# The rows of v go out behind the decay rows and the raw rows, in every item's step

## The chip, the cores and the metric

One core of a Trainium2 chip runs the whole program in one launch. The figure of merit is the device time of one execution in microseconds. The kernel before took 563.85 us (median of three runs, 561.96 to 565.06). TensorE (PE) multiplies, VectorE (DVE), ScalarE (ACT) and GpSimd (POOL) work elementwise, and SyncE (SP) does nothing here but issue transfers (DMAs).

## The reference

Causal attention with a decay bias over 4 batches of 8 heads (576 positions, 64 wide), then two dense stages, then a soft mixture of experts:

```
scores = q k^T / 8 + min(-(cum_i - cum_j), 0), causal     # cum = cumsum(max(s, 0))
x = softmax(scores) v                                     # 32 heads -> [2304, 512]
x = ((x w1) * (x w2)) w3 w_out                            # weights come in as 64 bit floats
logits = x phi;  slots = softmax(logits, tokens)^T x      # 32 slots, 8 experts
out = softmax(logits, slots) [relu(slots w1_e) w2_e]
```

## The kernel before, in words

**Items and steps.** Attention is cut into 40 items (`ITEMS`, L273): the 8 heads of batch 0 with query tiles 0 to 2, the same heads with tiles 3 and 4, and then 24 whole heads. `att_steps` (L645) writes down for step n, in this order: score products and the row maximum of item n (`att_scores`, L330), the division of item n-1 by its sums (`att_norm`, L363), the loads (the list `prep`), the transposes of item n-1, and in even steps the products with v for the pair n-2, n-1 (`att_pv`, L405).

**The loads of a step.** `att_values` (L293) issues the rows of v for a pair of heads and does so only when item n+1 is an odd head; it is one DMA on SP (L298), 320 KB for the first four pairs and 576 KB from then on. There are two buffers of v, so a v row waits until the products with v of two pairs earlier are done. `att_prep` (L301) of a later item (n+3 in the first items, n+1 from item 15 on) issues that item's decay rows: four short rows from a scratch tensor (L314), on SP, or on ACT's queue for items 16 to 23. From item 16 on it also splits the raw rows of q and k into a high and a low part: L319 and L321 on DVE, L325 and L322 on POOL, and one DMA on ACT's queue (L320). `att_fetch` (L275) issues the raw rows of q and k of an item one later still (n+4 in the first items, n+2 from item 14 on): one DMA (L290, 160 KB or 576 KB), or two for tiles 3 and 4 (L287, L288).

**What else is on SP.** The 64 bit weights come in as pieces called raw words (L178, 512 KB each, three buffers). ACT (L192, L203) and DVE (L195 to L199, L204, L207) turn them into 32 bit floats; `w12` pieces feed the dense stage, whose products are `glu_half` (L440, the matmuls at L447, the product of the two halves at L465). In the second half of the attention converted pieces go back out to a scratch tensor (L237). At the end 32 blocks of expert weights come in (L853, L868).

**What sets the order.** SP's instructions stand exactly as the program writes them (L64), and SP takes them one at a time: an issue that waits holds back all that are written behind it. On PE, DVE, ACT and POOL a scheduler sets the order when the program is built, from its own estimate of when each operand arrives. So a change on SP also moves instructions on the other engines. PSUM tiles come from three groups with 4, 2 and 2 banks (`PB`, L78); scores and dense products share the four.

Of the kernel before, what the change touches and what calls it, by code (L numbers as in the profile page):

```python
# [47 lines left out]
def attn_glu_softmoe_kernel(  # L48
# [226 lines left out]
    def att_fetch(n, ap):  # L275
        h, tiles = ITEMS[n]
        if h % 2 == 0:
            b, c = divmod(h // 2, H // 2)
            for blk, (_, nt, own) in enumerate(BLK):
                if own[0] in tiles:  # L280
                    x_t[b, blk, c] = xpl.tile([P, 2, nt], F32R, tag=f"x{blk}", name=f"x_{b}_{blk}_{c}", bufs=NX)
        q0, q1 = QT[tiles[0]][0], sum(QT[tiles[-1]])
        tag = ("raw", "qa", "qb")[n % 3] if n < NF32 else "raw"
        raw = ap.tile([P, 2, S], F32, tag=tag, name=f"raw_{n}", bufs=NRW)
        m = 64 if n < NF32 else P
        if q0:
            nc.sync.dma_start(raw[:m, 0, q0:q1], qk[h, 0, :m, q0:q1])  # L287
            nc.sync.dma_start(raw[:m, 1, :q1], qk[h, 1, :m, :q1])  # L288
        else:
            nc.sync.dma_start(raw[:m, :, :q1], qk[h, :, :m, :q1].rearrange("n p t -> p n t"))  # L290
        hd[n] = dict(raw=raw, q0=q0, q1=q1)

    def att_values(n, ap):  # L293
        h, tiles = ITEMS[n]
        if h % 2:
            vt = ap.tile([P, 9, 2, D], F32, tag="v", name=f"v_{n}", bufs=VB)
            nv = 2 * tiles[-1] + 1
            nc.sync.dma_start(vt[:, :nv], v[h // 2, :, :nv])  # L298
            hd[n]["v"] = hd[n - 1]["v"] = vt
# [30 lines left out]
    def att_scores(n, i, ap):  # L330
        t, tiles = hd[n], ITEMS[n][1]
        if i == tiles[0]:
            t["nmax"] = sm.tile([P, 6], F32, tag="nmax", name=f"nmax_{n}")
            t["rsum"] = rsum_t[n % 3]
            if n >= H or n % 2 == 0:
                t["sc"] = ap.tile([P, 1600], F32, tag="sc", name=f"sc_{n}", bufs=SCB)
            else:
                t["sc"] = hd[n - 1]["sc"][:, 800:]
        nmax, rsum, mul = t["nmax"], t["rsum"], t["mul"]
        q0, r = QT[i]  # L340
        W = q0 + r

        r = P
        sc = t["sc"][:, 64 * i * i : 64 * i * i + W]
        cuts = [(0, W)] if W <= 512 else [(0, W // 2), (W // 2, W)]
        for m, (a, z) in enumerate(cuts):
            pp = psum("sg", f"sc_ps_{n}_{i}_{m}")
            for x in mul:
                nc.tensor.matmul(pp[:r, : z - a], x[:, 0, q0 : q0 + r], x[:, 1, a:z], start=x is mul[0], stop=x is mul[-1])  # L349
            m0 = S - P if i == 0 else S - W + a  # L350
            last = m == len(cuts) - 1
            nc.vector.tensor_tensor_reduce(  # L352
                out=sc[:r, a:z], in0=pp[:r, : z - a], in1=hd["mask"][:r, m0 : m0 + z - a], scale=-0.125,
                scalar=3.0e38 if m == 0 else nmax[:r, 5:6], op0=ALU.add, op1=ALU.min,
                accum_out=nmax[:r, i : i + 1] if last else nmax[:r, 5:6],
            )
        nc.scalar.activation(  # L357
            out=sc[:r, :W], in_=sc[:r, :W], func=AF.Exp, bias=nmax[:r, i : i + 1], scale=-1.0,
            accum_out=rsum[:r, i, 0:1],
        )  # L360

    def att_norm(n):
        t, tiles = hd[n], ITEMS[n][1]  # L363
        rinv = sm.tile([P, 5], F32, tag="rinv", name=f"rinv_{n}")
        span = slice(tiles[0], tiles[-1] + 1)
        nc.vector.tensor_reduce(out=rinv[:, span], in_=t["rsum"][:, span], axis=AX.X, op=ALU.add)
        nc.vector.reciprocal(rinv[:, span], rinv[:, span])  # L367
        for i in tiles:
            sc = t["sc"][:, 64 * i * i : 64 * i * i + sum(QT[i])]
            nc.gpsimd.tensor_scalar(  # L370
                out=sc, in0=sc, scalar1=rinv[:, i : i + 1], scalar2=1.0, op0=ALU.mult, op1=ALU.mult
            )

    def att_transpose(n, i, ap):
        t = hd[n]
        tiles = [j for j in ITEMS[n][1] if j]
        if i == tiles[0]:
            t["pt"] = ap.tile([P, 10, P], F32, tag="pt", name=f"pt_{n}", bufs=PTB)
            t["ptd"] = ap.tile([P, 5, 64], F32, tag="ptd", name=f"ptd_{n}", bufs=PTB)
        pt, ptd = t["pt"], t["ptd"]  # L380
        W = sum(QT[i])
        sc = t["sc"][:, 64 * i * i : 64 * i * i + W]
        tp = psum("tp", f"pt_ps_{n}_{i}")
        for j in range(i):
            nc.tensor.transpose(tp[:, j * P : (j + 1) * P], sc[:, j * P : (j + 1) * P], ident)  # L385
        p0, step = PT[i]
        t["turned", i] = nc.scalar.copy(  # L387
            out=pt[:, p0 : p0 + step * (i - 1) + 1 : step], in_=tp[:, : i * P].rearrange("p (j q) -> p j q", q=P)
        )
        if i == tiles[-1]:  # L390


            dg = psum("tp", f"ptd_ps_{n}")
            own = [j for j in ITEMS[n][1] if j] + [0] * (ITEMS[n][1][0] == 0)
            for k in [len(own) - 1, *range(len(own) - 2, -1, -1)]:
                j = own[k]
                c0 = max(0, 64 * j * j + sum(QT[j]) - P)
                p0 = 64 * k + (64 if j == 0 else 0)
                nc.tensor.transpose(dg[:, p0 : p0 + P], t["sc"][:, c0 : c0 + P], ident)  # L399
                t["diag", j] = k  # L400
            t["turned", "d"] = nc.scalar.copy(out=ptd[:, : len(own)].rearrange("p j q -> p (j q)"), in_=dg[:, 64 : 64 * len(own) + 64])
# [244 lines left out]
    def att_steps(ap):  # L646

        groups = [[] for _ in range(B + 1)]
        N = len(ITEMS)
        for n in range(N + 1):  # L650
            tiles = ITEMS[n][1] if n < N else ()
            old = [i for i in ITEMS[n - 1][1] if i] if 0 < n <= N else []
            sc = [(0.2 + 0.3 * i, lambda i=i, n=n: att_scores(n, i, ap)) for i in tiles]
            tr = [(0.2 + 0.3 * i, lambda i=i, n=n: att_transpose(n - 1, i, ap)) for i in old]
            norm = [(0, lambda n=n: att_norm(n - 1))] if 0 < n <= N else []
            prep = [(0, lambda n=n: att_values(n + 1, ap))] if n + 1 < N else []
            d = FAR if n + FAR < NF32 else 1 if NF32 <= n + 1 < N else 0
            if d:
                prep += [(0, lambda m=n + d: att_prep(m, ap))]
            d = FAR + 1 if n + FAR + 1 < NF32 else 2 if NF32 <= n + 2 < N else 0  # L660
            if d:
                prep += [(0, lambda m=n + d: att_fetch(m, ap))]
            blks = [k for k in range(2) if BLK[k][2][0] in ITEMS[n - 1][1]]
            pv = [(1.4, lambda n=n, k=k: att_pv(n - 2, k)) for k in blks] if n > 0 and n % 2 == 0 else []
            groups[min(B, max(0, (n - 1) // H))] += [
                *sc[:1], *norm, *sc[1:2], *prep, *sc[2:3], *tr[:1], *sc[3:4], *tr[1:2], *sc[4:], *tr[2:], *pv
            ]
        return groups
# [78 lines left out]
    with tc.tile_pool(name="att", bufs=1) as ap:  # L747
# [14 lines left out]
        hd["mask"] = mask  # L762
        hd["ap"] = ap
        att = att_steps(ap)
        decay_rows()
        for n in range(NDIR):
# [20 lines left out]
        def load(k):  # L787
            i = k // 2 - 1
            if FC <= i < N0:
                (sum_rows if k % 2 else use_rows)(*TODO[i])  # L790
            if k < 2 * N0:
                load_words(k, ap)
            if k + NRAW < 2 * N0:
                fetch_words(k + NRAW, ap)
# [8 lines left out]
        prep = [(1, lambda k=k: load(k)) for k in range(2 * N0 + 2)]  # L803
# [15 lines left out]
        for b in range(2, B):  # L819
            steps, late = glu_steps(b - 1, late)  # L820
            n = len(more) // (B - b)
# [309 lines left out]
```

## Time and profile before

| | |
|---|---|
| median of 3 runs | 563.85 us (561.96 to 565.06) |
| profiled execution: time, span | 559.7 us, 557.9 us |
| PE busy | 517.9 us, 93% of the span |
| DVE, ACT, POOL busy | 319.6, 311.1, 199.4 us |
| granted TensorE clock, mean over the span | 0.987 of full |
| DMA | 118.03 MB, 212 GB/s over the span |

The profiled execution is 4.15 us shorter than the median of the runs. PE is the engine with the most work, so what matters is where PE stands idle, and where its clock is at the lower level. In the pages' lists a group stands for a line, an engine and an operation; the wait behind a row in brackets is the idle time of that engine just before the row, with what ended it.

### The profile page before, as it was taken

What the parts mean: (1) busy time and instruction counts of PE and PEld (TensorE: products, weight loads), DVE (VectorE), ACT (ScalarE), POOL (GpSimd) and SP (SyncE); (2) the same over time, 40 slices, a digit from 0 to 9 for tenths busy, and PEclk for the clock granted to TensorE, in tenths of its full rate; (3) what the DMA queues carried; (4) which work ended last, traced back from release to release, by engine and by line L of the source; (5) the groups of instructions that cost most, each with busy time, mean ns of one, the idle gap of its engine ahead of it and who ended that gap; (6) DMA issues with size and microseconds to landing.
All of it is one profiled execution on the core that took longest, in us unless ns stands there. A gap on an engine that the chain in (4) does not pass through costs nothing.

```text
span 557.9 us, 11842 instructions
## 1 busy us (share of the span) xinstructions
PE 517.9 (93%) x4288; PEld 432.6 (78%) x4288; DVE 319.6 (57%) x966; ACT 311.1 (56%) x845; POOL 199.4 (36%) x247
## 2 busy tenths in 40 slices
PE   3889899998989999999999799999999999999993
PEld 2566688787878989989999599898988999843452
DVE  7468787889984464855675648347640311243333
ACT  4585676889865666745776477557734211321222
POOL 5474554429755372434452434343310000000000
PEclk9997999999999999999999899999999999999998
DMA  5855965877554252655357337543530999689977
GB/s 154 239 162 174 289 210 200 300 239 264 204 180 151 85 149 93 172 188 157 129 179 244 123 98 202 178 151 118 172 125 20 407 413 385 236 282 424 420 305 243
DMA packets 38809, 118.03 MB, mean 212 GB/s; under 512 B 4224, under 2 KB 10560, under 8 KB 35296
## 3 DMA queue, kind: packets, MB, share of 16 engines
q1 hardware_dynamic: 36768, 113.60, 59.3%
q10 hardware_dynamic: 1984, 3.69, 2.5%
q8 instruction: 34, 0.56, 0.4%
q14 instruction: 23, 0.19, 0.1%
HBM read 102.11 MB, written 11.60 MB: 204 GB/s over the span
## 4 chain that ended last, share of the span: by engine, by line
PE 69%; DMA 13%; DVE 8%; issue 3%; ACT 2%; POOL 2%; SPq 1%; DVEq 0%; ACTq 0%; POOLq 0%
PE gl L447 30%; PE sc_ps L349 7%; PE x_ps L110 7%; DMA raw_w<-in_w 5%; PE pt_ps L385 5%; PE gn_ps L617 3%; PE o_ps L1032 3%; PE h_ps L994 3%; DMA raw<-in_qk 3%; PE ptd_ps L399 2%; PE z_ps L110 2%; DMA raw_wot<-in_wot 2%; DMA raw_w3t<-in_w3t 2%; PE lg L110 2%; POOL sc L370 1%
## 5 line engine op out<-in xcount | busy, mean ns | idle before, releaser
L447 PE MATMUL gl<-x,w12t 128*128 128x320 f32 (+1 forms) x1536 | 237.3, 304 | 4.0 <-DVE gU L465 3.0
L447 PEld LDWEIGHTS gl<-x,w12t 128*128 128x128 f32 x1536 | 212.3, 191 | 11.4 <-issue 4.0
L370 POOL TENSOR_SCALAR sc<-sc,rinv 128x64 f32<-128x64 f32 (+4 forms) x160 | 95.2, 613 | 48.3 <-DVE rinv L367 33.9
L357 ACT ACTIVATE sc<-sc,nmax 128x64 f32<-128x64 f32 (+4 forms) x160 | 89.5, 561 | 32.5 <-DVE nmax L352 31.6
L325 POOL TENSOR_TENSOR qa<-raw,qa 64x576 fp32r<-64x576 f32 x24 | 36.3, 1513 | 140.5 <-DVE qa L319 109.5
L352 DVE CUSTOM_DVE_ANT_0 sc<-sc_ps,mask 128x64 f32<-128x64 f32 (+4 forms) x160 | 64.8, 423 | 29.4 <-PE sc_ps L349 23.7
L387 ACT COPY pt<-pt_ps 128x128 f32<-128x128 f32 (+3 forms) x128 | 52.7, 424 | 34.5 <-PE pt_ps L385 20.1
L385 PE MATMUL pt_ps<-ident,sc 128*128 128x128 f32 x320 | 55.9, 283 | 5.1 <-ACT pt L387 2.5
L385 PEld LDWEIGHTS pt_ps<-ident,sc 128*128 128x128 f32 x320 | 38.4, 143 | 16.9 <-issue 8.1
L453 ACT COPY a<-gl 128x256 f32<-128x256 f32 (+1 forms) x64 | 25.3, 397 | 46.6 <-PE gl L447 37.0
L349 PE MATMUL sc_ps<-qa 128*128 128x64 f32 (+1 forms) x144 | 46.3, 334 | 5.0 <-DVE nmax L352 2.6
L110 PE MATMUL x_ps<-pt,v 128*64 128x256 f32 (+1 forms) x384 | 47.4, 353 | 0.0
L349 PE MATMUL sc_ps<-raw 68*128 68x288 f32 (+4 forms) x96 | 35.4, 513 | 11.2 <-DMA raw<-rows 9.6
L349 PE MATMUL sc_ps<-qb 68*128 68x64 f32 (+1 forms) x144 | 43.6, 306 | 0.0
L1003 POOL MEMSET ht<- 128x1024 f32 x2 | 1.9, 954 | 109.9 <-DVE ew L907 101.0
L322 POOL TENSOR_TENSOR qb<-raw,qa 64x576 fp32r<-64x576 f32 x24 | 37.7, 1572 | 2.2 <-PE gn_ps L617 0.5
L435 DVE TENSOR_TENSOR x<-x_ps,x 128x320 fp32r<-128x320 f32 (+1 forms) x32 | 13.9, 451 | 42.7 <-ACT x L434 42.6
L110 PEld LDWEIGHTS x_ps<-pt,v 128*64 128x64 f32 x384 | 33.2, 138 | 5.4 <-issue 1.3
L349 PEld LDWEIGHTS sc_ps<-qa 128*128 128x128 f32 x144 | 27.4, 190 | 8.8 <-DVE nmax L352 4.1
L349 PEld LDWEIGHTS sc_ps<-raw 68*128 68x128 f32 x96 | 21.1, 258 | 16.8 <-issue 12.6
L192 ACT ACTIVATE w_w<-raw_w 128x512 f32<-128x512 f32 x32 | 21.6, 676 | 19.4 <-DMA raw_w<-in_w 18.1
L357 ACT ACTIVATION_READ_ACCUMULATOR sc<-sc,nmax 128x1 f32 x160 | 30.6, 191 | 0.0
(180 smaller groups left out, 788.6 us busy)
## 6 DMA issues: line engine op xcount, KB each, us to landing
ew<-in_ew SPq DMA_DIRECT2D x27, 1024.0 KB
raw_w<-in_w SPq DMA_DIRECT2D x32, 512.0 KB
raw<-in_qk SPq DMA_DIRECT2D x24, 576.0 KB
v<-in_v SPq DMA_DIRECT2D x16, 576.0 KB
raw_w3t<-in_w3t SPq DMA_DIRECT2D x16, 512.0 KB
raw_wot<-in_wot SPq DMA_DIRECT2D x8, 512.0 KB
raw_wo<-in_wo SPq DMA_DIRECT2D x8, 512.0 KB
w_d<-w_w SPq DMA_DIRECT2D x8, 512.0 KB
```

What stands on the lines that cost most here:

```text
L110: mm = nc.tensor.matmul(out_, lhs, rhs, start=start, stop=stop)
L192: line_up(nc.scalar.activation(out=w, in_=hi.bitcast(F32), func=AF.Copy, scale=F64_SCALE))
L322: nc.gpsimd.tensor_tensor(out=qb[0:64, 1, :q1], in0=rk[0:64, :q1], in1=qa[0:64, 1, :q1].bitcast(F32), op=ALU.subtract)
L325: nc.gpsimd.tensor_tensor(out=qa[64:, 0, q0:q1], in0=rq[64:, q0:q1], in1=qa[64:, 0, q0:q1].bitcast(F32), op=ALU.subtract)
L349: nc.tensor.matmul(pp[:r, : z - a], x[:, 0, q0 : q0 + r], x[:, 1, a:z], start=x is mul[0], stop=x is mul[-1])
L352: nc.vector.tensor_tensor_reduce(out=sc[:r, a:z], in0=pp[:r, : z - a], in1=hd["mask"][:r, m0 : m0 + z - a], scale=-0.125, scalar=3.0e38 if ...
L357: nc.scalar.activation(out=sc[:r, :W], in_=sc[:r, :W], func=AF.Exp, bias=nmax[:r, i : i + 1], scale=-1.0, accum_out=rsum[:r, i, 0:1],)
L370: nc.gpsimd.tensor_scalar(out=sc, in0=sc, scalar1=rinv[:, i : i + 1], scalar2=1.0, op0=ALU.mult, op1=ALU.mult)
L385: nc.tensor.transpose(tp[:, j * P : (j + 1) * P], sc[:, j * P : (j + 1) * P], ident)
L387: t["turned", i] = nc.scalar.copy(out=pt[:, p0 : p0 + step * (i - 1) + 1 : step], in_=tp[:, : i * P].rearrange("p (j q) -> p j q", q=P))
L447: nc.tensor.matmul(acc[:, :nt], w12_t[fc][:, wi, n, kc], x_t[b, blk, kc][:, xi], start=k == 0, stop=k == 3 * KC - 1)
L453: st["a_copy"] = nc.scalar.copy(out=a_sb[:, :nt], in_=acc[:, :nt])
```

## The change

The call of `att_values` moves from the front of the list `prep` to its back. Which transfers are made, what they wait for and how large they are stays as it was; only the order on SP differs, and with it the order that the scheduler gives to the other engines.

```
-            prep = [(0, lambda n=n: att_values(n + 1, ap))] if n + 1 < N else []
+            prep = []
             d = FAR if n + FAR < NF32 else 1 if NF32 <= n + 1 < N else 0
             if d:
                 prep += [(0, lambda m=n + d: att_prep(m, ap))]
             d = FAR + 1 if n + FAR + 1 < NF32 else 2 if NF32 <= n + 2 < N else 0
             if d:
                 prep += [(0, lambda m=n + d: att_fetch(m, ap))]
+            prep += [(0, lambda n=n: att_values(n + 1, ap))] if n + 1 < N else []
```

Behind the inserted line all line numbers of the changed kernel are one higher.

**SP in step 4**, before (`raw_310` is item 7, `raw_360` item 8, `v_356` the pair 4 and 5, `raw_w_3_0` a piece of words of w1 and w2):

```order
L178 DMA raw_w_2_1_324<-in_w 128x512
L298 DMA v_356<-in_v 128x640
L314 DMA raw_310<-rows_d 4x2x320
L287 DMA raw_360<-in_qk 64x256
L288 DMA raw_360<-in_qk 64x576
L178 DMA raw_w_3_0_388<-in_w 128x512
```

and now:

```order
L178 DMA raw_w_2_1_324<-in_w 128x512
L314 DMA raw_310<-rows_d 4x2x320
L287 DMA raw_358<-in_qk 64x256
L288 DMA raw_358<-in_qk 64x576
L298 DMA v_361<-in_v 128x640
L178 DMA raw_w_3_0_388<-in_w 128x512
```

The v row has moved past three rows and stands right before the piece of words. In later steps it moves past two rows (L314 and L290), and past L290 alone where ACT issues the decay rows.

**DVE some steps later**, before (the conversion of the pieces `w_w_3_0` and `w_w_3_1`, and the scores of item 8, tiles 3 and 4):

```order
L195 TENSOR_SCALAR w_w_3_0_551<-w_w_3_0_551 128x512
L196 SCALAR_TENSOR_TENSOR w_w_3_0_551<-raw_w_3_0_388,w_w_3_0_551 128x512
L435 TENSOR_TENSOR x_0_1_155<-x_ps_0_390,x_0_1_155 128x320
L352 ISA sc_561,nmax_560<-sc_ps_3_0_562,mask 128x448
L352 ISA nmax_560 128x1
L199 SCALAR_TENSOR_TENSOR w_w_3_0_551<-raw_w_3_0_388,w_w_3_0_551 128x512
L352 ISA sc_561,nmax_560<-sc_ps_4_0_572,mask 128x288
L352 ISA nmax_560 128x1
L195 TENSOR_SCALAR w_w_3_1_600<-w_w_3_1_600 128x512
L352 ISA sc_561,nmax_560<-sc_ps_4_1_575,mask,nmax_560 128x288
```

and now:

```order
L195 TENSOR_SCALAR w_w_3_0_551<-w_w_3_0_551 128x512
L196 SCALAR_TENSOR_TENSOR w_w_3_0_551<-raw_w_3_0_388,w_w_3_0_551 128x512
L366 TENSOR_REDUCE rinv_566<-rsum_94 128x3
L199 SCALAR_TENSOR_TENSOR w_w_3_0_551<-raw_w_3_0_388,w_w_3_0_551 128x512
L367 RECIPROCAL rinv_566<-rinv_566 128x3
L195 TENSOR_SCALAR w_w_3_1_600<-w_w_3_1_600 128x512
L196 SCALAR_TENSOR_TENSOR w_w_3_1_600<-raw_w_3_1_439,w_w_3_1_600 128x512
L199 SCALAR_TENSOR_TENSOR w_w_3_1_600<-raw_w_3_1_439,w_w_3_1_600 128x512
L352 ISA sc_561,nmax_560<-sc_ps_3_0_562,mask 128x448
```

Both conversions now stand in front of the scores of item 8.

**DVE and PE in step 33**, before (`raw_4018` is item 34 behind `v_4006`; `gl_1_7_1` and `gl_0_0_0` are dense products, `z_ps` the product that sums up the slots). DVE:

```order
L352 ISA sc_3987,nmax_3986<-sc_ps_4_1_4065,mask,nmax_3986 128x288
L352 ISA nmax_3986 128x1
L546 RECIPROCAL mx_0_0_3897<-mx_0_0_3897 64x1
L546 RECIPROCAL mx_0_1_3905<-mx_0_1_3905 128x2
L547 TENSOR_TENSOR c_all<-c_all,mx_0_0_3897 64x32
L547 TENSOR_TENSOR c_all<-c_all,mx_0_1_3905 128x64
L319 CAST qa_4205<-raw_4018 128x576
L321 CAST qa_4205<-raw_4018 128x576
```

and now, where the split of item 34 stands in front of the last scores of item 33:

```order
L319 CAST qa_4205<-raw_4016 128x576
L321 CAST qa_4205<-raw_4016 128x576
L545 TENSOR_SCALAR mx_0_0_3897<-mx_0_0_3897 64x1
L545 TENSOR_SCALAR mx_0_1_3905<-mx_0_1_3905 128x2
L352 ISA sc_3987,nmax_3986<-sc_ps_4_1_4065,mask,nmax_3986 128x288
```

PE at the same place, before:

```order
L349 MATMUL sc_ps_2_0_4214<-qb_4008 128x320
L447 MATMUL gl_0_0_0_4219<-x_0_0_2267,w12t_201 128x320 x3
L447 MATMUL gl_0_0_0_4219<-x_0_1_2586,w12t_201 128x320 x3
L447 MATMUL gl_0_0_0_4219<-x_0_2_2920,w12t_201 128x320 x3
L110 MATMUL z_ps_0_4025<-gn_0_0_3641,dT_0_3950 32x512 x2
L399 MATMUL ptd_ps_3959<-ident,sc_3603 128x128 x5
```

and now:

```order
L349 MATMUL sc_ps_2_0_4214<-qb_4006 128x320
L110 MATMUL z_ps_0_4025<-gn_0_0_3641,dT_0_3950 32x512 x2
L110 MATMUL z_ps_0_4025<-gn_0_1_3745,dT_0_3950 32x512 x2
L110 MATMUL z_ps_0_4025<-gn_0_2_3805,dT_0_3950 32x512 x2
L399 MATMUL ptd_ps_3959<-ident,sc_3603 128x128 x5
L385 MATMUL pt_ps_1_4035<-ident,sc_3819 128x128
L447 MATMUL gl_0_0_0_4219<-x_0_0_2265,w12t_201 128x320 x3
```

The six products of `z_ps` and the transposes behind them now stand in front of the first dense product of the next block.

## Rows read from the trace of the kernel before

**Rows 1.** Windows: length, busy us of PE, PEld, DVE, ACT, POOL, clock, DMA share, GB/s.
```profile
20.00:180.00 160.00, 148.63 (x1147) 121.02 (x1145) 126.85 (x349) 117.12 (x322) 89.66 (x96) 0.98 0.69 221
80.00:100.00 20.00, 20.00 (x130) 16.60 (x130) 13.89 (x40) 15.38 (x38) 9.62 (x10) 1.00 0.58 202
180.00:300.00 120.00, 120.00 (x1025) 111.19 (x1024) 74.27 (x245) 77.96 (x224) 55.18 (x70) 1.00 0.47 146
```
**Rows 2.** Waits of SP: line, releaser, total us, times, longest us.
```profile
SPq L298 <- PE x_ps L110: 83.5, 11, 16.3
...
SPq L314 <- PE sc_ps L349: 25.9, 8, 5.8
```
**Rows 3.** Waits of DVE for the raw rows: total us, times, longest us.
```profile
DVE qa L319 <- DMA raw<-in_qk: 12.0, 6, 5.1
```
**Rows 4.** Timeline: one of these splits, with DVE's idle time before it.
```profile
95.61 0.46 DVE L319 CAST qa<-raw 128x576 fp32r<-128x576 f32 x1 [1.46 <-DMA raw<-in_qk]
```
**Rows 5.** Timeline of SP in step 33.
```profile
295.75 0.44 SPq L298 DMA_DIRECT2D v<-in_v  x1
...
296.67 0.38 SPq L290 DMA_DIRECT2D raw<-in_qk  x1
```
**Rows 6.** The chain that ended last, at the same place.
```profile
296.67 8.52 DMA raw<-in_qk
```
**Rows 7.** Windows at the same place, columns as in rows 1.
```profile
300.00:304.00 4.00, 4.00 (x36) 4.00 (x35) 0.22 (x2) 2.75 (x7) 0.00 (x0) 1.00 1.03 397
310.00:316.00 6.00, 5.40 (x26) 2.96 (x26) 3.13 (x12) 0.55 (x2) 3.21 (x4) 0.72 0.45 141
```
**Rows 8.** Timeline of DVE at the same place.
```profile
305.31 0.46 DVE L319 CAST qa<-raw 128x576 fp32r<-128x576 f32 x1 [5.09 <-DMA raw<-in_qk]
...
308.00 2.21 DVE L207 SCALAR_TENSOR_TENSOR w_w<-raw_w,w_w 128x512 int32<-128x512 int32 x1
```
**Rows 9.** Timeline of PE at the same place.
```profile
306.81 0.36 PE L349 MATMUL sc_ps<-qa 128*128 128x192 f32 x1 [1.02 <-DVE gU L465]
...
310.60 2.49 PE L447 MATMUL gl<-x,w12t 128*128 128x320 f32 x9 [3.00 <-DVE gU L465]
313.02 1.70 PE L110 MATMUL z_ps<-gn,dT 128*32 128x512 f32 x4
```
**Rows 10.** Timeline of SP, DVE and PE around step 21.
```profile
148.21 2.63 SPq L178 DMA_DIRECT2D raw_w3t<-in_w3t  x2
152.08 0.33 SPq L298 DMA_DIRECT2D v<-in_v  x1
152.46 0.43 SPq L290 DMA_DIRECT2D raw<-in_qk  x1
...
158.97 0.46 DVE L319 CAST qa<-raw 128x576 fp32r<-128x576 f32 x1 [2.25 <-DMA raw<-in_qk]
...
160.00 0.41 PE L349 MATMUL sc_ps<-qa 128*128 128x320 f32 x1 [0.76 <-DVE nmax L352]
```
**Rows 11.** A window there, columns as in rows 1.
```profile
152.00:158.00 6.00, 4.56 (x52) 3.88 (x52) 4.72 (x9) 4.80 (x14) 3.84 (x8) 1.00 0.96 302
```
**Rows 12.** Timeline of SP, DVE and PE around step 4.
```profile
33.28 0.33 SPq L298 DMA_DIRECT2D v<-in_v  x1
...
35.67 0.51 SPq L178 DMA_DIRECT2D raw_w<-in_w  x1
...
33.58 0.87 DVE L199 SCALAR_TENSOR_TENSOR w_w<-raw_w,w_w 128x512 uint32<-128x512 uint32 x1
...
42.93 0.61 DVE L352 CUSTOM_DVE_ANT_0 sc<-sc_ps,mask 128x448 f32<-128x448 f32 x1
...
45.95 1.64 DVE L199 SCALAR_TENSOR_TENSOR w_w<-raw_w,w_w 128x512 uint32<-128x512 uint32 x1
...
44.56 3.62 PE L349 MATMUL sc_ps<-raw 68*128 68x448 f32 x6 [1.34 <-DVE nmax L352]
```
**Rows 13.** A window there, columns as in rows 1.
```profile
44.00:52.00 8.00, 7.44 (x26) 5.30 (x28) 6.30 (x19) 4.50 (x13) 3.08 (x3) 0.57 0.54 171
```

More of the change, by code (lines that the diff above doesn't have):

```diff
@@ L655, in att_steps @@
             norm = [(0, lambda n=n: att_norm(n - 1))] if 0 < n <= N else []
-            prep = [(0, lambda n=n: att_values(n + 1, ap))] if n + 1 < N else []
+            prep = []
             d = FAR if n + FAR < NF32 else 1 if NF32 <= n + 1 < N else 0
@@ L662, in att_steps @@
                 prep += [(0, lambda m=n + d: att_fetch(m, ap))]
+            prep += [(0, lambda n=n: att_values(n + 1, ap))] if n + 1 < N else []
             blks = [k for k in range(2) if BLK[k][2][0] in ITEMS[n - 1][1]]
```

## The prediction

> **What bounds the kernel now.** I read the trace in this order: windows of PE's busy time along the span, then the waits of SP and of DVE, then the timeline where DVE waits for raw rows. The windows show where time can be had at all. From 180 to 300 us PE is busy 120.00 of 120 us at full clock, and so it is from 80 to 100; from 20 to 180 it stands idle 160 - 148.63 = 11.4 us, nearly all of it outside that stretch [rows 1]. An operand that comes earlier pays only where PE has gaps; beside a full PE it pays nothing.
>
> The waits show how much the v rows hold back. SP stands at L298 for 83.5 us in 11 waits for products with v, the longest 16.3 us, with the decay rows and raw rows of the step queued behind it [rows 2]. DVE in turn idles 12.0 us in six places until raw rows land [rows 3]; in five of the six (items 16, 22, 24, 30 and 34) the awaited row is one that SP issues behind a v row. The first is item 16 [rows 4], the largest item 34: SP issues v at 295.75 and the raw rows at 296.67 [rows 5], they land 8.52 us later [rows 6], and DVE has then been idle for 5.09 us [rows 8].
>
> **The change part by part.** Nothing is added or removed: 20 v issues of some 0.4 us move past one to three rows each, all on SP's queue; ACT's queue and POOL keep their issues. I price three places and set the rest to nothing.
>
> *Step 33, items 33 and 34.* SP is not held here (v goes out at 295.75, the raw rows 0.92 us later), so the earlier issue counts for little; what counts is the data in front. v is 576 KB, 0.59 MB; the DMA engines move 397 GB/s with a busy share of 1.03 from 300 to 304 us [rows 7], so without v ahead the raw rows land 0.59 / 0.397 = 1.5 us sooner. DVE's chain behind L319 then ends 1.5 us sooner, and PE's two gaps of 1.02 and 3.00 us [rows 9], both ended by DVE's L465 behind that chain, shrink by that much. PE's new order adds something: the z_ps products, whose first four take 1.70 us from 313.02 [rows 9], stand in front of gl_0_0_0 and can run while PE waits for L465. They in turn wait for L600 and L604 behind L207, so I count 1.0 us of them. Sum 2.5 us. The bounds are 0 (v and the raw rows share the engines, and DVE's L319, now earlier in its order, holds up the last scores) and 4.0 for both gaps plus the lower clock behind them: 6 us at a mean of 0.72 [rows 7] lose 6 x 0.28 = 1.7 us. I take the clock as lost again, because a single gap of 1.34 us, with smaller ones ahead of it, was enough in the early stretch [rows 12, 13], where the clock is 0.57 on average over 8 us, which is 3.4 us lost, part of the time at 1.2 GHz.
>
> The Trainium skill ("TensorE: Matmul & The Clock Gate", section "What's actually happening") says of the clock that "the default state is throttled, and activity releases the throttle"; by that rule a shorter gap could keep the full 2.4 GHz, and the sum below would be 1.7 us larger, at 558.4. The trace bears it out in part: two gaps with 4.02 us in 5 us were followed by the lower level [rows 7, 9], and the idle 1.4 us between 152 and 158 were not, at a granted clock of 1.00 [rows 11].
>
> *Step 21, item 22.* SP ends its words issue at 148.21 + 2.63 = 150.84, stands until v goes out at 152.08, and issues the raw rows at 152.46 [rows 10]. Now they can go at about 150.9, 1.5 us earlier, if POOL has let go of the buffer by then, as I take it; and 0.59 MB less in front at 302 GB/s [rows 11] is another 2.0 us. That is more than DVE's idle 2.25 us ahead of L319, so this wait goes [rows 10]. On PE only the gap of 0.76 us that follows, which waits for DVE's scores, is tied to it [rows 10]: 0.8 us. Bounds 0 and 2.25.
>
> *The early stretch, steps 4 to 9.* A v row waits here too, and three rows stand between it and the next piece of words: v at 33.28, words at 35.67 [rows 12]. Now the words follow v directly. They also wait for DVE's conversion of an older piece (L199, 33.58 + 0.87 = 34.45 [rows 12]), so they go at 34.5, 1.2 us sooner. The words sit on the chain, but DVE's new order puts both conversions before the scores of item 8, which takes part of it back, so I count 0.5 us. Above, the gap of 1.34 us [rows 12] and the 3.4 us of lower clock [rows 13] could go, 4.7; below it can cost 4.2, worked out under the third rival.
>
> *At nothing:* the waits for items 16, 24 and 30, since PE is full or nearly full around them [rows 1]; without that cover they would give up to 12.0 - 5.09 - 2.25 = 4.7 us [rows 3, 8, 10]. v itself goes out later, by the rows now in front, 1 to 2 us, or where the decay rows wait for scores (L314, at most 5.8 us [rows 2]) by that. Its buffer is filled for products that come a pair of items, tens of us, later in the second half, so I see no new wait of PE; what stands behind v on SP (words, stores) moves with it, and L178 and L237 mostly wait for DVE anyway. In the last third of the span nothing changes.
>
> Sum: 2.5 + 0.8 + 0.5 = 3.8 us. Against the profiled execution of 559.7 that is 555.9; this one is 4.15 us below the median of the runs, so the time that I state is 563.85 - 3.8 = 560.05, 560.1.
>
> **The rivals.** The bound for a difference is 0.5%, 2.8 us, about what a measurement of this kernel can tell from no change.
>
> *The waits were covered.* What SP lost was mostly beside a full PE [rows 1]; in the second half the decay rows wait for scores anyway [rows 2], which come later in PE's order than the products that v waits for, so the rows behind them gain little; and the changed order in step 33 uses up what the data gain. Then only item 22 is left: 563.85 - 0.8 = 563.1. Against it speaks that two of the five places lie directly in front of PE gaps.
>
> *The order in the queue does nothing.* v and the raw rows might share the DMA engines evenly instead of following each other, so that the change does not do what it says where SP is not held; then the raw rows of step 33 gain half, 0.75 us, and z_ps half of its 1.0: 563.85 - 1.25 - 0.8 - 0.5 = 561.3. For it speaks that 8.52 us is more than the 3.0 us that v and the raw rows together take at 397 GB/s [rows 6, 7]; against it, that the program writes pieces of words in front of both, whose data may explain the rest.
>
> *Slower: the early order.* DVE now converts two pieces before it reads item 8's scores. Before, that read began at 42.93 and the second conversion ended at 45.95 + 1.64 = 47.59 [rows 12]; should the words come no earlier than now, the read starts at that end, less the three reads of at most 0.61 us that stood in between: 47.59 - 42.93 - 1.8 = 2.8 us later. PE, which stood 1.34 us for this bank, stands 2.8 us longer, and the stretch at 1.2 GHz [rows 13] grows by that, half of which is lost: 2.8 + 1.4 = 4.2. With DVE's L319 in step 33 too early in its order as well, the 2.5 are gone and 0.8 stay: 563.85 + 4.2 - 0.8 = 567.2. It decides once the cost there is over 3.6 us, which needs words that land no sooner than before. For it speaks that the reordering rests on estimated arrivals; against it, that the words are issued 1.2 us sooner.
>
> **How the numbers follow.** My case (rows earlier, PE's gaps shorter) 0.43, with a range of its own from 556.5 to 561.0; the waits were covered 0.28; the queue's order does nothing 0.07; slower 0.22. The first lies below 561.0, the second and third within 0.5% of 563.85, the fourth above 566.7 but for a small part, so faster 0.43, same 0.36, slower 0.21. If all three places came out at their upper ends the time would be some 12 us lower, which I hold for unlikely; the range goes to 555.0, and up to 567.5 to take in the third case.
>
> **What would show it.** Right: SP's waits at L298 stay about as long but the raw rows stand in front of them; DVE's idle time for raw rows falls from 12.0 to under 5 us; in step 33 the raw rows land at most 7.5 us after their issue and PE's two gaps together fall from 4.0 to under 2.5 us; PE's idle time between 20 and 180 us is below 11 us. Wrong: PE's idle time up to 60 us grows, with a longer stretch below full clock, or the waits for raw rows go and PE's idle time stays, or new waits of PE for v appear.

## The result, and the profile after

The change made the kernel slower: 567.7 us (median of 14 runs, 564.23 to 571.94) against 562.4 us (14 runs, 559.56 to 565.36), a ratio of 1.0094 with a 95% interval of 1.0067 to 1.0122. The profiled execution took 569.28 us, its span is 567.5 us. The two profiled executions lie further apart than the medians, 9.6 us of time and of span against 5.3 us: that of the kernel before is 2.7 us below its median, that of the changed kernel 1.6 us above.

On SP the rows changed places as forecast. The first two rows are waits of SP (total us, times, longest us), the third the wait of DVE for raw rows:

```profile
SPq L314 <- PE sc_ps L349: 59.9, 10, 15.8
...
SPq L298 <- PE x_ps L110: 40.9, 9, 10.4
...
DVE qa L319 <- DMA raw<-in_qk: 4.0, 1, 4.0
```

The decay rows now wait first (59.9 us instead of 25.9), and v waits half as long for products with v (40.9 us instead of 83.5), which was not forecast [rows 2]; DVE's idle time for raw rows fell from 12.0 us to 4.0 [rows 3]. Steps 21 and 33 in the timeline of the changed kernel (start, length, engine or queue, line; in brackets the idle time before it):

```profile
160.04 0.39 SPq L290 DMA_DIRECT2D raw<-in_qk  x1
165.20 0.33 SPq L298 DMA_DIRECT2D v<-in_v  x1
...
166.63 0.45 DVE L319 CAST qa<-raw 128x576 fp32r<-128x576 f32 x1
...
307.41 0.38 SPq L290 DMA_DIRECT2D raw<-in_qk  x1
307.88 0.42 SPq L298 DMA_DIRECT2D v<-in_v  x1
...
314.71 0.46 DVE L319 CAST qa<-raw 128x576 fp32r<-128x576 f32 x1 [4.05 <-DMA raw<-in_qk]
...
316.18 0.55 PE L594 MATMUL dt_ps<-ident,lT 128*128 128x128 f32 x3 [1.42 <-ACT pt L387]
...
317.31 1.85 PE L447 MATMUL gl<-x,w12t 128*128 128x256 f32 x10 [0.34 <-DVE nmax L352]
...
321.69 1.91 PE L110 MATMUL z_ps<-gn,dT 128*32 128x512 f32 x12
```

In step 33 DVE takes the raw rows 7.30 us after their issue (the transfer took 8.52 us before [rows 6]), and PE stands 1.42 + 0.34 = 1.76 us instead of 4.02 [rows 9]. In step 21 DVE no longer waits [rows 10].

The loss is earlier. Of the 192 score reads of DVE (L352), counted from 0, the 12th comes 2.0 us later than before, the 24th (item 8's first) 5.9, the 27th (item 9's first) 9.4 and the 99th to the 144th 11.1 to 11.5; step 33 then gives some 2 to 2.5 back, and the last third keeps +9.6. Here is the early stretch, first of the kernel after, then of the kernel before:

```profile
35.94 0.34 SPq L298 DMA_DIRECT2D v<-in_v  x1
36.38 0.37 SPq L178 DMA_DIRECT2D raw_w<-in_w  x1
...
38.40 0.53 SPq L178 DMA_DIRECT2D raw_w<-in_w  x1
...
52.60 0.33 SPq L298 DMA_DIRECT2D v<-in_v  x1
53.05 0.37 SPq L178 DMA_DIRECT2D raw_w<-in_w  x1
...
45.10 0.68 ACT L192 ACTIVATE w_w<-raw_w 128x512 f32<-128x512 f32 x1 [1.31 <-DMA raw_w<-in_w]
...
48.25 0.69 DVE L199 SCALAR_TENSOR_TENSOR w_w<-raw_w,w_w 128x512 uint32<-128x512 uint32 x1
48.86 0.61 DVE L352 CUSTOM_DVE_ANT_0 sc<-sc_ps,mask 128x448 f32<-128x448 f32 x1
...
39.52 0.85 PE L399 MATMUL ptd_ps<-ident,sc 128*128 128x128 f32 x3
...
42.51 3.75 PE L349 MATMUL sc_ps<-raw 68*128 68x448 f32 x6 [1.93 <-issue]
...
57.78 0.85 PE L399 MATMUL ptd_ps<-ident,sc 128*128 128x128 f32 x3
...
63.08 0.49 PE L399 MATMUL ptd_ps<-ident,sc 128*128 128x128 f32 x3
```

```profile
25.85 0.85 PE L399 MATMUL ptd_ps<-ident,sc 128*128 128x128 f32 x3
...
35.32 0.55 PE L399 MATMUL ptd_ps<-ident,sc 128*128 128x128 f32 x3 [0.23 <-ACT pt L387]
37.67 0.49 PE L399 MATMUL ptd_ps<-ident,sc 128*128 128x128 f32 x3
...
40.83 1.96 PE L349 MATMUL sc_ps<-raw 68*128 68x448 f32 x6
...
42.54 0.69 ACT L192 ACTIVATE w_w<-raw_w 128x512 f32<-128x512 f32 x1 [0.69 <-DMA raw_w<-in_w]
```

Two things are to be seen. Item 8's first scores are read at 48.86, behind both word conversions, 5.9 us later than before [rows 12]. And three equal transposes (L399) still take 0.85 us at 57.78 in the kernel after, and 0.49 us from 63.08; before, they took 0.49 us at 37.67 already. Six equal score products (L349) take 3.75 us at 42.51 after, and 1.96 us at 40.83 before. TensorE first rose from 1.2 to 2.4 GHz some 24 us later. The column of the granted clock does not show this: up to the first change of the clock that the trace records (34.5 us before, 58.7 after) it stands at 1.00, whatever the matmuls take. So the busy time there has to be split by hand. Windows of both kernels, before first (columns as in rows 1), the last row of each being the whole span:

```profile
0.00:34.50 34.50, 21.46 (x76) 16.38 (x77) 22.24 (x85) 19.52 (x61) 18.06 (x38) 1.00 0.60 171
44.70:51.50 6.80, 6.80 (x20) 4.73 (x20) 5.13 (x15) 3.79 (x10) 2.58 (x3) 0.50 0.54 173
310.90:314.30 3.40, 3.40 (x13) 1.97 (x11) 1.79 (x5) 0.00 (x0) 2.31 (x3) 0.51 0.23 92
0.00:557.90 557.90, 517.93 (x4288) 432.60 (x4288) 319.62 (x966) 311.13 (x845) 199.36 (x247) 0.99 0.62 212
```

```profile
20.00:180.00 160.00, 145.80 (x1020) 119.53 (x1020) 123.82 (x336) 111.90 (x302) 85.40 (x90) 0.98 0.69 214
180.00:300.00 120.00, 119.56 (x1047) 108.78 (x1042) 68.33 (x225) 76.38 (x220) 54.17 (x70) 1.00 0.47 144
...
0.00:58.70 58.70, 41.95 (x143) 29.92 (x144) 32.60 (x117) 30.57 (x93) 27.91 (x52) 1.00 0.54 163
75.80:79.20 3.40, 3.40 (x14) 3.22 (x13) 2.85 (x8) 2.26 (x7) 3.40 (x4) 0.50 0.77 236
157.70:161.10 3.40, 3.40 (x19) 3.07 (x19) 3.37 (x9) 2.21 (x9) 3.40 (x6) 0.50 0.46 158
318.10:321.50 3.40, 3.40 (x18) 3.33 (x16) 3.37 (x12) 2.70 (x7) 0.90 (x3) 0.51 0.00 0
0.00:567.50 567.50, 525.80 (x4288) 440.26 (x4288) 319.97 (x966) 312.26 (x845) 197.98 (x247) 0.99 0.62 208
```

I take half of PE's busy time at 1.2 GHz as lost against 2.4 GHz; that is an estimate (of the equal work above the scores lose 48%, the transposes 42%). Before that is (21.46 + 6.80 + 3.40) / 2 = 15.8 us, after (41.95 + 3 x 3.40) / 2 = 26.1 us. PE's idle time is 557.90 - 517.93 = 40.0 and 567.50 - 525.80 = 41.7 us. What remains, the work at full clock, is 502.1 and 499.7. So of 9.6 us between the two executions 10.3 are lost at the lower clock and 1.7 in idle time, with 2.4 less in the rest. The split is of these two executions; the medians are 5.3 us apart. The same split for other kernels of this study, each from its own windows:

| kernel (profiled execution) | span | idle | lost at 1.2 GHz | rest | first rise at |
|---|---|---|---|---|---|
| before | 557.9 | 40.0 | 15.8 | 502.1 | 34.5 |
| before, second profile | 558.5 | 40.3 | 16.7 | 501.6 | 42.7 |
| after | 567.5 | 41.7 | 26.1 | 499.7 | 58.7 |
| after, second profile | 566.3 | 39.5 | 27.8 | 499.0 | 57.3 |
| v last in step 0 alone | 574.6 | 41.8 | 31.1 | 501.8 | 62.4 |
| after, with seven blocks of filler | 567.5 | 41.7 | 15.6 | 510.2 | 38.2 |
| new queue, engines in the old order | 558.3 | 37.2 | 21.0 | 500.1 | 48.7 |
| the same, new order at step 33 | 553.3 | 35.3 | 16.5 | 501.5 | 43.5 |
| new queue, all but TensorE in the old order | 559.6 | 35.8 | 22.1 | 501.7 | 56.8 |
| new queue, TensorE alone in the old order | 556.4 | 35.0 | 20.0 | 501.4 | 43.8 |
| v last before step 14 alone | 569.8 | 42.4 | 25.5 | 501.9 | 35.8 (lower again from 39.2 to 49.4) |
| v last from step 20 on alone | 555.2 | 39.7 | 12.6 | 503.0 | 34.7 |
| v last in step 32 alone | 557.3 | 37.2 | 18.9 | 501.1 | 44.1 |
| after, item 8 held behind the second product | 570.1 | 44.7 | 23.6 | 501.8 | 37.4 (lower again from 40.8 to 57.9) |
| v last in step 0 alone, item 8 held behind it | 571.5 | 46.7 | 25.0 | 499.8 | 49.2 |

In all these kernels but the one with filler the rest lies between 499.0 and 503.0 us: their spans differ by idle time and by time lost at the lower clock, and where the first rise stands is not all of the latter.

### The profile page after: what moved, and what is told of

Same layout as the page of the kernel before. It is cut to its first block, busy times and chain, and to the rows that moved or that the text cites. A ratio compares the mean times of both kernels' runs of the same rounds, so it can differ in the third digit from the quotient of the medians.

```text
span 567.5 us, 11852 instructions
## 1 busy us (share of the span) xinstructions
PE 525.8 (93%) x4288; PEld 440.3 (78%) x4288; DVE 320.0 (56%) x966; ACT 312.3 (55%) x845; POOL 198.0 (35%) x247
## 4 chain that ended last, share of the span: by engine, by line
PE 67%; DMA 13%; DVE 10%; ACT 4%; issue 3%; SPq 0%; POOL 0%; DVEq 0%; ACTq 0%
PE gl L447 29%; PE x_ps L110 7%; PE sc_ps L349 7%; DMA raw_w<-in_w 5%; PE pt_ps L385 4%; PE gn_ps L617 3%; PE o_ps L1033 3%; PE h_ps L995 3%; PE ptd_ps L399 3%; DMA raw<-in_qk 2%; DMA raw_w3t<-in_w3t 2%; PE z_ps L110 2%; DVE sc L352 2%; PE lg L110 2%; DMA rows_d<-rows 1%
## 5 line engine op out<-in xcount | busy, mean ns | idle before, releaser
L447 PE MATMUL gl<-x,w12t 128*128 128x320 f32 (+1 forms) x1536 | 240.2, 305 | 3.4 <-DVE nmax L352 2.7
L370 POOL TENSOR_SCALAR sc<-sc,rinv 128x64 f32<-128x64 f32 (+4 forms) x160 | 93.8, 604 | 61.4 <-DVE rinv L367 46.7
L352 DVE CUSTOM_DVE_ANT_0 sc<-sc_ps,mask 128x64 f32<-128x64 f32 (+4 forms) x160 | 64.7, 423 | 30.8 <-PE sc_ps L349 24.4
L349 PE MATMUL sc_ps<-raw 68*128 68x288 f32 (+4 forms) x96 | 39.4, 561 | 14.8 <-DMA raw<-rows 9.6
L349 PE MATMUL sc_ps<-qa 128*128 128x64 f32 (+1 forms) x144 | 46.5, 337 | 5.1 <-DVE nmax L352 3.8
L385 PEld LDWEIGHTS pt_ps<-ident,sc 128*128 128x128 f32 x320 | 39.5, 145 | 13.1 <-issue 8.1
L453 ACT COPY a<-gl 128x256 f32<-128x256 f32 (+1 forms) x64 | 25.4, 398 | 43.8 <-PE gl L447 40.2
L349 PE MATMUL sc_ps<-qb 68*128 68x64 f32 (+1 forms) x144 | 43.8, 308 | 0.0
L349 PEld LDWEIGHTS sc_ps<-raw 68*128 68x128 f32 x96 | 22.7, 277 | 21.7 <-issue 15.2
L110 PEld LDWEIGHTS x_ps<-pt,v 128*64 128x64 f32 x384 | 34.6, 144 | 4.7 <-issue 1.3
L322 POOL TENSOR_TENSOR qb<-raw,qa 64x576 fp32r<-64x576 f32 x24 | 37.4, 1559 | 1.7
L349 PEld LDWEIGHTS sc_ps<-qa 128*128 128x128 f32 x144 | 27.7, 193 | 8.3 <-DVE nmax L352 4.9
L620 ACT COPY gn<-gn_ps 128x512 f32<-128x512 f32 x40 | 22.7, 582 | 16.0 <-PE gn_ps L617 15.6
```

The lines of the kernel that those rows point to most:

```text
L110: mm = nc.tensor.matmul(out_, lhs, rhs, start=start, stop=stop)
L322: nc.gpsimd.tensor_tensor(out=qb[0:64, 1, :q1], in0=rk[0:64, :q1], in1=qa[0:64, 1, :q1].bitcast(F32), op=ALU.subtract)
L352: nc.vector.tensor_tensor_reduce(out=sc[:r, a:z], in0=pp[:r, : z - a], in1=hd["mask"][:r, m0 : m0 + z - a], scale=-0.125, scalar=3.0e38 if ...
L370: nc.gpsimd.tensor_scalar(out=sc, in0=sc, scalar1=rinv[:, i : i + 1], scalar2=1.0, op0=ALU.mult, op1=ALU.mult)
L447: nc.tensor.matmul(acc[:, :nt], w12_t[fc][:, wi, n, kc], x_t[b, blk, kc][:, xi], start=k == 0, stop=k == 3 * KC - 1)
L453: st["a_copy"] = nc.scalar.copy(out=a_sb[:, :nt], in_=acc[:, :nt])
```

## The experiments

Ratios are to the kernel before, run on the same chip, with 95% intervals.

**Which steps.** One condition decides in which steps v goes last; `behind` was `n < 14`, `n >= 20`, `n == 32`, `n == 0`, and `n in (2, 6, 10, 12, 18)`:

```
-            prep = []
+            prep = [(0, lambda n=n: att_values(n + 1, ap))] if n + 1 < N and not behind else []
...
-            prep += [(0, lambda n=n: att_values(n + 1, ap))] if n + 1 < N else []
+            prep += [(0, lambda n=n: att_values(n + 1, ap))] if n + 1 < N and behind else []
```

> The rows of v are issued last only in the steps before step 14; from step 14 on they are issued first, as before. Observed in the changed kernel's profile: its score reads run +2.8 us behind the kernel before at the 21st, +9.4 at the 27th and +11.5 from the 99th on, and step 33 gives 2.5 back. Theory A (clock): TensorE's first rise to the full clock slips from about 34 us to about 59 us in the trace, and that is most of the loss. Theory B (order and queue): the scores wait behind word conversions and late rows, and the clock only goes along. Both expect here the loss without the gain of step 33: ratio to the kernel before 1.016 to 1.022, about 573 us. If the loss came from later steps instead, the ratio is 0.997 to 1.005.

Measured 1.0242 (1.0200 to 1.0284), above the expectation: the early steps carry the loss, and more of it than the full change has.

> The rows of v are issued last only from step 20 on, so the first 400 TensorE rows stand in the order of the kernel before. Theories A and B both expect the early loss gone and the gains of step 33 (2.5 us) and of step 20 (up to 0.8 us) kept: ratio 0.994 to 0.997, first rise of the clock at about 34 us as in the kernel before. If the engines' order in steps 20 on (43 to 355 lines of it differ) costs something of its own, the ratio is 1.000 or above.

Measured 0.9984 (0.9961 to 1.0007), between the two expectations; the first rise is at 34.7 us. The loss is gone and little is gained. The two halves do not add up to the whole: 1.0242 x 0.9984 is 1.023, and the full change has 1.0094. Each build gets an order of its own from the scheduler, so such parts cannot be summed.

> The rows of v are issued last in step 32 alone; all engines' rows up to TensorE's 1009th stand as in the kernel before. If the gain of step 33 that the changed kernel's profile shows (TensorE idle between the 144th and the 156th score read 1.8 instead of 4.0 us, and 0 to 1.7 us less at the lower clock) stands alone: ratio 0.993 to 0.997, about 558. If it is taken back behind it: 0.998 to 1.002.

Measured 0.9972 (0.9943 to 1.0001), some 1.6 us: at the upper edge of the first expectation, with an interval that just touches no change.

> The rows of v are issued last in step 0 alone (one DMA of 20 changes its place), which already makes the scheduler write TensorE's rows 28 to 436 and VectorE's 54 to 378 in another order; three score matmuls of item 8 then stand ahead of the second product with v. Theory C: most of the early loss is there, ratio 1.008 to 1.022, and the fourth issue of v (40.6 us in the kernel before, 52.6 in the changed one) comes after 46 us. Theory D: one DMA later by 2 us costs at most that, ratio 0.998 to 1.004.

Measured 1.0231 (1.0181 to 1.0282), the fourth v at 49.3 us. One DMA of twenty, issued 1.4 us later, costs more than twice what the whole change does. The rewritten order of the engines is what else differs. That the order costs the time, and not this DMA's data, this run alone does not show; it had no twin with the order held.

> The rows of v are issued last in steps 2, 6, 10, 12 and 18 alone, the five in which this leaves the order on TensorE as it was (6 of its 1803 rows move; 36 lines on VectorE). Theory C (engines' order): the loss of the early stretch comes from the order that the scheduler writes for TensorE and VectorE, not from the place of v in SP's queue: ratio 0.997 to 1.004, the 27th score read within 2 us of the kernel before, first rise of the clock at 34 to 36 us. Theory D (queue): rows and v landing in another order cost the time themselves; five of the ten early moves then bring a third or more of the early 11.5 us: ratio 1.006 to 1.012.

Measured 1.0028 (0.9993 to 1.0064): five moves that leave the engines' order nearly alone cost next to nothing, as theory C has it, though the first rise of the clock came at 42.1 us and not at 34 to 36. Both results speak for theory C.

**Filler for TensorE.** Transposes of the identity into a tile that nothing reads, at the end of a step:

```
+    def fill(n):
+        f = psum("acc", f"fill_{n}")
+        for j in range(8):
+            nc.tensor.transpose(f[:, j % 4 * P : (j % 4 + 1) * P], ident, ident)
...
+            more_pe = [(0, lambda n=n: fill(n))] if n in (2, 3, 4, 5, 6, 7, 8) else []
...
-                *sc[:1], *norm, *sc[1:2], *prep, *sc[2:3], *tr[:1], *sc[3:4], *tr[1:2], *sc[4:], *tr[2:], *pv
+                *sc[:1], *norm, *sc[1:2], *prep, *sc[2:3], *tr[:1], *sc[3:4], *tr[1:2], *sc[4:], *tr[2:], *pv, *more_pe
```

> The changed kernel, and in each of steps 2 to 8 eight transposes of the identity into a PSUM tile that nothing reads: work for TensorE that waits for no rows and no conversion (56 transposes, 13 us at the lower clock by 0.9 us for three plus overlap, 6.6 us at the full one, part of it in idle time). Theory A: the clock rises before 45 us instead of at 59, the 27th score read comes at 50 to 54 us instead of 58.7, and the kernel is at least 3 us faster than the changed kernel: ratio to the kernel before 0.996 to 1.004. Theory B: the clock may rise sooner, but the 27th score read stays at 57 us or later and the ratio is 1.009 to 1.02.

Measured 1.0208 (1.0165 to 1.0252). Its timeline of PE:

```profile
32.16 1.97 PE L649 MATMUL fill<-ident 128*128 128x128 f32 x8
...
38.28 1.04 PE L649 MATMUL fill<-ident 128*128 128x128 f32 x8
...
40.24 0.49 PE L399 MATMUL ptd_ps<-ident,sc 128*128 128x128 f32 x3
```

The clock does rise at 38 us, the 27th score read comes at 53.7 us, and the time lost at 1.2 GHz falls by 10.5 us to 15.6, as theory A has it; but the rest grows by 10.5 (56 fillers at 1.04 / 8 us are 7.3 of it, the other 3.2 are not accounted for), so the span is the same and the runs are slower than either theory had it. The gain was spent on the filler, so this run does not show that an early rise by itself makes the kernel faster.

> The changed kernel with eight transposes of the identity in step 2 alone (about 2 us of work for TensorE at the lower clock, 1 us at the full one). With seven such blocks the first rise of the clock came at 38 us instead of 59, and about 10 us less was lost at the lower clock, while 8 us of filler were added. Theory A (the lower clock is what the time is lost to): one block gets the early rise (before 45 us) for 1 to 2 us: at least 4 us faster than the changed kernel, ratio to the kernel before 0.997 to 1.003. Theory B (order alone): the ratio stays at 1.008 or above even where the clock rises early.

Measured 1.0062 (1.0028 to 1.0097), between the two expectations. The clock rose at 36.7 us and was at the lower level again from 40.1 to 57.2: 21.9 us lost at 1.2 GHz. Intervals overlap with the changed kernel's, so this only points the way of theory A.

> The kernel before with the same 56 extra transposes in steps 2 to 8. Theory A: the lower clock between 44 and 51 us of the kernel before (about 3.5 us lost in it) goes away or the first rise comes before 34 us; ratio 0.993 to 1.000. Theory B: the extra work only adds, 2 to 6 us: ratio 1.003 to 1.010.

Measured 1.0129 (1.0095 to 1.0162): in the kernel before the filler only adds, beyond what was expected.

> A try at a faster kernel: v last in step 32 alone (ratio 0.9972), and six transposes of the identity at the end of step 4, where TensorE of the kernel before stood for 1.34 us at 43 us and then ran at the lower clock from 45 to 52 us. If work in that gap keeps the clock up: 1 to 3 us less than step 32 alone, ratio 0.991 to 0.996. If the clock falls elsewhere or the extra work (0.8 to 1.5 us) costs as much: 0.997 to 1.003.

Measured 0.9972 (0.9937 to 1.0007), no better than step 32 alone.

**One rule of order.** In the changed kernel four of six score products of items 8 and 9 stand ahead of the second product with v on TensorE; v's fourth issue waits for that product (52.60 us above), with words behind it. A dependence that only orders was added:

```
+                if n in {8: 2} and i == tiles[0] and m == 0:
+                    tc.add_manual_dep(mm.ins, st["pv", {8: 2}[n]].ins.name, NoSync, reason="order")
```

> The changed kernel with one rule of order more: the first score matmul of item 8 stands behind the last matmul of the second product with v (items 2 and 3) on TensorE. v stays last in every step. TensorE's rows up to the 170th then stand as in the kernel before but for 16 lines; VectorE and ScalarE keep most of the changed kernel's order. Theory C (the place of the second product with v, which sets when the fourth v, and the words queued behind it on SP, are issued): the fourth v is issued at 42 to 45 us instead of 52.6, the loss of the early stretch goes and the gain of step 33 stays: ratio to the kernel before 0.993 to 1.002. If VectorE's order or the place of v in the queue makes the loss, it stays: 1.006 to 1.012.

> v last in step 0 alone (ratio 1.0231 without more), and item 8's first score matmul behind the second product with v as in the run beside it. TensorE then differs from the kernel before in 14 lines of order, VectorE in 92. Theory C: ratio 0.997 to 1.005, the fourth v issued before 45 us. Otherwise 1.012 or more.

Measured 1.0187 (1.0151 to 1.0224) and 1.0204 (1.0161 to 1.0246). Theory C in this narrow form fell: the fourth v went out at 47.8 and 47.9 us, between the 40.6 of before and the 52.6 of the changed kernel, and the loss stayed. Timeline of the second kernel (lines are six higher there):

```profile
43.94 0.66 ACT L193 ACTIVATE w_w<-raw_w 128x512 f32<-128x512 f32 x1 [2.45 <-DMA raw_w<-in_w]
44.50 0.35 ACT L393 COPY pt<-pt_ps 128x256 f32<-128x256 f32 x1
...
45.00 0.45 PE L391 MATMUL pt_ps<-ident,sc 128*128 128x128 f32 x1 [2.10 <-ACT pt L393]
```

ACT takes its queue in order: it stands 2.45 us for words that have not landed, a copy that PE needs waits behind it, and PE stands 2.10 us. Putting one row right let the scheduler move others, DVE's and ACT's among them; PE's idle time in these two kernels is 44.7 and 46.7 us against 40.0 before.

**Queue and order apart.** At the end of the kernel each engine's instructions are chained, without any wait, in the order that another build has:

```
+    for row in ORDERS:                     # one list of instruction numbers for each engine
...
+        for i, j in zip(ids, ids[1:]):
+            tc.add_manual_dep(nc.get_inst_by_name(f"I-{j}"), f"I-{i}", pin, reason="order")
```

The kernel before, chained in its own order, is the same program instruction for instruction, so the chain adds nothing by itself. The reverse combination, the old queue with the new order, was not run: by the two orders it would deadlock, since the new order has scores ahead of a product with v whose rows the old queue issues behind a v that waits for that product.

> SP's queue as in the changed kernel, with v last in every step; the instructions of TensorE, VectorE, ScalarE and GpSimd each held in the order of the kernel before by order-only dependences (a table of their numbers), so that no row of these engines differs from it. Theory C (the engines' order makes the loss): the early loss goes, and rows of queries and keys come sooner at step 33: ratio to the kernel before 0.993 to 1.000. Theory D (the queue makes it): 1.006 to 1.015.

Measured 0.9911 (0.9876 to 0.9946), 556.9 against 561.75 us. Its timeline at items 8 and 9 and at step 33 (the profiled execution, 560.1 us, is one of the longer ones of this kernel):

```profile
48.90 0.62 DVE L352 CUSTOM_DVE_ANT_0 sc<-sc_ps,mask 128x448 f32<-128x448 f32 x1 [1.14 <-PE sc_ps L349]
...
53.58 0.60 DVE L352 CUSTOM_DVE_ANT_0 sc<-sc_ps,mask 128x448 f32<-128x448 f32 x1
...
300.84 0.38 SPq L290 DMA_DIRECT2D raw<-in_qk  x1
301.31 0.42 SPq L298 DMA_DIRECT2D v<-in_v  x1
...
307.96 0.46 DVE L319 CAST qa<-raw 128x576 fp32r<-128x576 f32 x1 [2.89 <-DMA raw<-in_qk]
...
313.26 1.58 PE L447 MATMUL gl<-x,w12t 128*128 128x320 f32 x9 [2.03 <-DVE gU L465]
```

The data come 1.5 us sooner after their issue than before (307.96 - 300.84 = 7.1 against 305.31 - 296.67 = 8.6 [rows 5, 8]), and of PE's two gaps one of 2.03 us is left, with no order changed on PE. That is the queue's part by itself. The early lines show that an item 8 read late is not yet the loss: 48.90 is as late as in the changed kernel (48.86), but item 9's first scores come at 53.58, 4.3 us later than before and not 9.4.

> As the run before, but with the engines' order of the kernel that has v last in step 32 alone: as before up to TensorE's 1009th row, and behind it as in the changed kernel for 30 lines. Theory C: ratio 0.991 to 0.998, at or under the run before, and under 0.9972 if the early queue order by itself also helps. Theory D: 1.006 to 1.015.

Measured 0.9884 (0.9839 to 0.9929), 555.3 against 561.75: the lowest ratio of the study, though its interval overlaps with that of the run before.

> SP's queue as in the changed kernel, TensorE alone held in the order of the kernel before; VectorE keeps 198, ScalarE 134 and GpSimd 24 lines of another order from the scheduler. If TensorE's order makes the loss: ratio 0.993 to 1.002. If it is where VectorE and ScalarE take the word conversions, ahead of the score reads and copies that TensorE waits for (the run with item 8 behind the second product with v shows ScalarE and VectorE standing for words): 1.008 to 1.022.

Measured 0.9988 (0.9956 to 1.0019).

> SP's queue as in the changed kernel; VectorE, ScalarE and GpSimd held in the order of the kernel before, TensorE left to the scheduler (some 75 lines of its order differ from the kernel before). If the place of the word conversions on VectorE and ScalarE makes the loss: ratio 0.993 to 1.002. If TensorE's order makes it: 1.006 to 1.015.

Measured 0.9972 (0.9946 to 0.9999).

This settles what the change of the queue is worth by itself: 0.9911, a gain of 5.0 us. The order that the scheduler writes in answer to it costs the other way, 1.0094 / 0.9911 = 1.018, some 10 us (8 to 13 by the two intervals).

Whether one engine's order makes the loss, the last two runs do not tell. Both have the loss gone but not the full gain; yet an engine that is not held does not keep the changed kernel's order, for the scheduler writes it anew. By the order of the records in the traces some 75 of TensorE's 4288 matmuls stand elsewhere than in the kernel before when the other three engines are held, against some 820 in the changed kernel; and when TensorE is held, some 185 of VectorE's 966 instructions stand elsewhere than in the changed kernel.

The split above says where the 10 us go, as far as single executions can. From the new queue with the old order to the changed kernel's two profiles, idle time grows by 2.3 and 4.5 us and the loss at 1.2 GHz by 5.1 and 6.8. The queue by itself takes some 3 us of idle time away (37.2 against 40.0 and 40.3). So the equal idle time of the kernels before and after is a gain and a loss that cancel, and the lower clock is the larger part of the order's price but not all of it.

**Is the late clock the kernel's or the execution's.**

> The changed kernel once more, for a second profile. If the late first rise of the clock belongs to its order: a rise at 50 us or later, or as much time lost at the lower clock by other stretches (20 us or more of the span in all, by half of TensorE's busy time there). If it was that execution's: a rise at 34 to 46 us and 13 to 18 us lost.

> The kernel before once more (its engines held in their own order, which leaves the program as it was), for a second profile. If its early rise belongs to its order: 33 to 46 us and 13 to 19 us lost at the lower clock in all. If the first profile was a lucky one: over 46 us, 20 us or more lost.

Second profiles of the two kernels, each a single run (568.1 and 560.35 us). PE in the changed kernel, then in the kernel before:

```profile
55.82 0.85 PE L399 MATMUL ptd_ps<-ident,sc 128*128 128x128 f32 x3
61.12 0.49 PE L399 MATMUL ptd_ps<-ident,sc 128*128 128x128 f32 x3
```

```profile
38.83 0.85 PE L399 MATMUL ptd_ps<-ident,sc 128*128 128x128 f32 x3
44.58 0.49 PE L399 MATMUL ptd_ps<-ident,sc 128*128 128x128 f32 x3
```

The rises are at 57.3 and 42.7 us, the losses at 1.2 GHz 27.8 and 16.7 us. The late rise belongs to the changed kernel and not to one execution of it. That the engines' order alone sets it is not shown: with the new queue and the old order the rise is at 48.7 us, between the two.

## Why the prediction was wrong

**Step 33: the size was right, one of its two terms was not.** 2.5 us was counted; PE's two gaps shrank by 2.26 us, and the lower clock behind them was lost again as assumed (318.10 to 321.50 at 0.51). In the run with the old order the gap is 2.03 us and no such stretch follows. The v rows in front were worth 1.5 us there (8.6 against 7.1), as counted, and PE's gaps shrank by 1.99 us without any new order. The 1.0 us for the z_ps products did not come as counted: in the changed kernel they run at 321.69, behind both gaps, and the gaps that are left wait for ACT and for DVE's L352, no longer for L465.

**Step 21: the wait went, as said** (2.25 us of DVE, and the 0.76 us of PE behind it). What it gave cannot be told apart, because the order around it changed too: PE now stands 1.83 us for DVE's L352 at 157.02, before that place.

**The early stretch: this is the step that failed.** I counted +0.5 us, on words issued 1.2 us sooner against an order that "takes part of it back". The words went out at 36.38 us instead of the 34.5 that I had worked out, since v itself waited until 35.94 for its product; the next pair went out at 53.05 instead of 42.99. In the run with the old order too the words went out at 36.13, behind a v at 35.70: the 1.2 us came with neither order. What weighed more is the term for the scheduler's answer. It was counted at 1.2 - 0.5 = 0.7 us and measured at some 10 us (1.018).

**The sum over the queue had the right sign and size.** With the engines held in their order, the queue gained 5.0 us (interval 3.0 to 7.0). Of the 3.8 us of the sum, 1.0 us was for TensorE's new order at step 33, which that run leaves out; 2.8 us are left, just under the interval. The first two rivals left the queue less, 0.8 and 2.6 us. Where the 5.0 us arise was looked at in step 33 alone, so that the sum came near may be luck in part.

**The rival of the early order had the place and the sign**, but it was held at 0.22 and reached its price by another way, so that its 567.2 is close to 567.7 is luck. I priced PE's gap at 2.8 us longer and the clock at 1.4. In fact item 8's scores came 5.9 us later, PE's idle time over the span stayed (41.7 and 39.5 against 40.0 and 40.3 us), and 10 to 11 us went at 1.2 GHz. The condition for it, words that land no sooner than before, was met: ACT takes the second piece at 45.10 us, after a wait for it, and took it at 42.54 before.

**Why I did not see the price.** I read the clock from its column, which is 1.00 before the first recorded change, and, but for two short stretches of lower clock, PE's idle time as all there was to win or lose. In the kernel before, 21.46 us of busy time up to 34.5 us ran at half speed, so a later rise was the largest thing that an early reordering could touch; the transposes at 0.85 and 0.49 us in the same trace show it.

**The signs that I named** split as the cause does: raw waits 4.0 us (under 5), landing 7.30 us (under 7.5), gaps 1.76 us (under 2.5) came out right; SP's waits at L298, which were to stay about as long, halved where they are for products with v (40.9 us against 83.5); PE's idle time from 20 to 180 us is 160 - 145.80 = 14.2 us, not below 11, and a longer stretch below full clock, named as a sign against, is there.

What stays open: which rows of the order hold the clock down, and whether they stand on one engine. The runs show that the place of the second product with v does not account for the loss.

## What to carry to other kernels

Where a scheduler orders the engines, a move on one queue is two changes; price them apart, and hold the engines' order while you test the queue. Here the queue was worth -0.9% and the new order +1.8%. Where TensorE does the most work, split its busy time by clock level first, from the durations of equal matmuls and not from the clock's column alone: idle time said "no difference" where 10 us were lost at the lower clock, because the queue's gain hid what idle time the new order added.

## What the runs showed of the hardware

The first rise to 2.4 GHz came at 34.5 and 42.7 us in two executions of one program, and at 58.7 and 57.3 in two of the other, so it scatters by some 8 us and still differs between the two. Two kernels that share the early order of the first (v last from step 20 on, and in step 32 alone) rose at 34.7 and 44.1 us. Before it rose in the second profile of the kernel before, PE had been busy 23.23 of the 24.0 us from 18.7 on; in the second of the kernel after, 35.57 of 38.6.

The Trainium skill ("TensorE: Matmul & The Clock Gate", section "What's actually happening") holds the ramp to be under 1% of a typical kernel's span. Here half of 21.46 us is 1.9% of 557.9, and half of 41.95 is 3.7% of 567.5; the measurement decides.
